# A long convolution beside a gated MLP: the taps' product on GpSimd, and the head, third stage and last stores rearranged

## The chip, the core and the metric

The kernel runs on one core of a Trainium2 chip. The metric is the device time in microseconds of one execution; the median of three runs is compared. Each core has five engines that run their own instruction queues in order and wait for one another by semaphores: TensorE (PE, matmuls from SBUF into PSUM), VectorE (DVE), ScalarE (ACT), GpSimd (POOL) and SyncE (SP, which here only issues DMAs).

## What is computed

```python
def reference(A_q, A_k, A_v, A_shift_k, A_ssm_k, A_ssm_D, B_x, B_w_gate, B_w_up, B_w_down):
    def _A_ref(q, k, v, shift_k, ssm_k, ssm_D):      # S = 2048, D = 640, ks = 4
        k_shift = sum(k_pad[:, t:t + S, :] * shift_k[:, ks - 1 - t] for t in range(ks))
        kv = k_shift * v
        y = irfft(rfft(kv, 2 * S) * rfft(ssm_k, 2 * S))[:S]      # a causal convolution over the sequence
        y = y + kv * ssm_D
        return q * y
    def _B_ref(x, w_gate, w_up, w_down):              # F = 1728
        return (sigmoid(x @ w_gate) * (x @ w_up)) @ w_down
    x = A_q
    xn = _layernorm(x, axis=-1)
    return x + _A_ref(xn, A_k, A_v, A_shift_k, A_ssm_k, A_ssm_D) + _B_ref(xn, B_w_gate, B_w_up, B_w_down)
```

(shortened: the sum over `t` is a loop, and the transforms are 2-d calls on a unit axis). All inputs are bf16.

## The kernel before

Two parts that share little run interleaved, so that TensorE always has something to do.

**The MLP.** The 2048 rows are 16 row blocks of 128 (`m`), in four groups of four (`tr`). The blocks are loaded into `acc`, which also collects the result. For each block the statistics are taken (`bn_stats` on VectorE, L629, or sums on ScalarE, L636 and L642), the rows are normalised into `xn` (L673, L675), transposed to `xnT` (on TensorE for groups 0 and 1, by DMA for 2 and 3), multiplied with the gate and up weights (`rec_first` at L732 for the first 256 columns of the first group, `rec_fc` at L751 for the rest), passed through sigmoid and product (`rec_evac`) into `hT`, and multiplied with the down weights (`rec_down`, L765). The step `fin` (L771) adds the down product from PSUM to `acc`.

**The convolution.** It is done as a transform in two factors over the sequence, in ten steps (`idx` 0 to 9, 16 channels of each of 4 groups a step). In each step, `rec_kv` makes the taps' sum on VectorE: two tap products of 2048 columns (L485), a sum of 2048 (L490), one of 1024 (L491), and then the product of the taps with `v` (L495, kind `ttkt`), which lands in one of two `kvt` buffers. `rec_st1` transforms `kvt` (and the filter `ht`) on TensorE (L513) and copies the result from PSUM to `T` (kind `ev_T`). `rec_st2` is the second factor (L533, `ev_S` into `S`), `rec_prod` the complex product on VectorE (L556 to L564; in steps 3 to 9 a swap DMA brings the halves together), `rec_st3` the inverse of the second factor (L574, `ev_V` into V, which is in VX). When all ten steps are through, `rec_st4` does the last factor (L604), and `ymul`, `yadd` (L611, L612) multiply with the normalised rows and add to `acc`. At the end `store` (L620) writes `acc` out.

**The order.** The code records some 900 operations with what they read and write. `ORDER` is a list, written out by hand or by a planner, of the numbers of these operations; they are emitted in just this order, each on its own engine, so it sets the order on every engine and on both DMA-issuing queues (SyncE and ScalarE). An operation that can run on two engines runs on the first that is listed unless its number is in `ON_DVE`. Buffers (`SLOTS`) are given out in the order of emission.

**Places that the change touches.** `sraw`, the raw shift taps, is one of the `EARLY` names, which live in the part of the tile VX that V's second half takes over later; it is written on every 32nd partition by `load_shift` (memset at L407, DMA at L408) and read by the matmuls `csh` (L414). The scratch of `bn_stats` (`bss`) and the normalised rows `xns` lie there too. `Ab` holds the constants of the third stage: three variants, of which `rec_st3` uses the third. `ROWS` names the steps in which the product `ttkt` writes rows: it reads with a step of 16 elements and writes contiguously.

Of the kernel before, what the change touches and what calls it, by code (L numbers as in the profile page):

```python
# [13 lines left out]
U16 = mybir.dt.uint16  # L14
I32 = mybir.dt.int32
ACT = mybir.ActivationFunctionType
# [3 lines left out]
DM = 640  # L20
# [22 lines left out]
def _dft_tables():  # L43
# [20 lines left out]
    A = np.zeros((2, K2, 3, N2, 2))  # L64
    A[0, :, 0, :, 0], A[0, :, 0, :, 1] = c, s
    A[1, :, 0, :, 0], A[1, :, 0, :, 1] = -c, -s
    A[:, :, 1, :, 0], A[:, :, 1, :, 1] = -s[None], c[None]
    A[0, :, 2, :, 0], A[0, :, 2, :, 1] = c, s
    A[1, :, 2, :, 0], A[1, :, 2, :, 1] = -s, c
    A = np.concatenate([A.reshape(P, 3 * N2 * 2), F], axis=1)  # L70
# [50 lines left out]
]  # L121
ON_DVE = [
    48, 98, 100, 104, 134, 135, 136, 137, 142, 145, 260, 325, 427, 439, 451, 474, 479, 486, 498, 503, 777, 826, 831,
    864, 867, 870, 873, 874, 875, 877, 878, 879, 880, 883, 886, 887, 888, 889, 890, 891, 892, 893, 894, 895
# [7 lines left out]
class _Plan:  # L132
# [47 lines left out]
    def table(self):  # L180
        other = set(ON_DVE)
        for i in ORDER:
            o = self.ops[i]
            o.on = [e for e in ("PE", "ACT", "DVE", "SP") if e in o.engs][i in other]
        return [self.ops[i] for i in ORDER]
# [45 lines left out]
def kernel(  # L231
# [17 lines left out]
    oq4 = out.flatten_outer_dims().rearrange("(n q m) d -> q n m d", q=4, m=NQ)  # L249
# [22 lines left out]
    At = cst.tile([P, 6 * N2 + 2 * K1], U16, name="At")  # L272
    Mb = Mt.bitcast(F16)
    Atb = At.bitcast(F16)
    Ab = Atb[:, 0:6 * N2].rearrange("p (x n) -> p x n", x=3)
    Fb = Atb[:, 6 * N2:6 * N2 + 2 * K1]
# [36 lines left out]
    EARLY = {"xn0", "xn1", "xn2", "xn3", "sraw", "jk", "ident", "FR", "w0_4", "bs0", "bs1", "bs2", "bs3"}  # L313
# [56 lines left out]
    ROWS = tuple(range(10))  # L370
    TD = 1
    FIN2 = (15,)
# [31 lines left out]
    def load_shift():  # L404
        b, c = "sraw", "csh"
        sr = lambda: tl[b].rearrange("p m d -> p (m d)")
        plan.op("memset_s", {"DVE": lambda: nc.vector.memset(sr()[:, 0:4 * CG], 0.0)}, w=[(b, 0)], alloc=[(b, "xq")])  # L407
# [65 lines left out]
    def rec_kv(idx):  # L473
# [8 lines left out]
        def mul(t, r):  # L482
# [12 lines left out]
        dve("ttkt", 1024, lambda: nc.vector.tensor_tensor(out(), f(tl[a][:, 0]), f(tl[vb][:, :, j0:j0 + 2 * JS]), ALU.mult),  # L495
            r=[(a,)] + vr_, w=[(o,)], alloc=[(o, "kvt")])
# [69 lines left out]
    def rec_st3(idx):  # L566
        half, sub = divmod(idx, NSUB)
        V, Z, S_ = f"V{half}", f"P{idx}", f"S{idx}"
        for b in range(2):
            c = f"c3_{idx}_{b}"  # L570

            def f(b=b, c=c):
                for j in range(JS):
                    nc.tensor.matmul(tl[c][:, j // 4, 128 * (j % 4):128 * (j % 4) + 128], lhsT=tl[S_][:, b, 0, j, :],  # L574
                                     rhs=Ab[:, 2, :], start=True, stop=True)
            z = (sub, b) == (0, 0)
            pe("st3", 8, f, r=[(S_, "z"), (S_, "q"), ("A",)] + ([] if z else [(V, "a")]),
               w=[(c,)] + ([(V, "a")] if z else []), alloc=[(c, "c")] + ([(V, "VA" if half == 0 else "VB")] if z else []))
            co = 2 * sub * JS + b
            ev("ev_V", 1024, lambda co=co: tl[V].rearrange("p n r d -> p (n r) d")[:, :, co:co + 2 * JS - 1:2],  # L580
               lambda c=c: tl[c].rearrange("p a n -> p (a n)").rearrange("p (j n) -> p n j", j=JS),
               r=[(c,)], w=[(V, sub, b)])
# [311 lines left out]
```

## Time and profile before

| what | us |
|---|---|
| median of 3 runs | 242.99 (242.56 to 243.24) |
| the profiled execution | 242.73 |
| its span (first to last instruction) | 240.7 |
| TensorE busy | 230.0 (granted clock 0.997) |
| VectorE busy | 194.3 |
| ScalarE busy | 182.3 |
| GpSimd busy | 0.7 |
| product `ttkt` (L495): 10 instructions on VectorE | 2.16 each |
| eviction `ev_V` (L355 into VX) on ScalarE | 1.30 each |
| `fin` (L771): 640 columns, 320 columns | 0.82, 0.49 |

A line of the profile names line, engine, operation and tiles (output first), then count, busy time, mean duration in ns, and after the last bar the idle time of the engine before these instructions with what ended it. In the chain and in timelines the first two numbers are start and duration in us. The 2.03 us between the span and the time of the execution lie outside of the program's own instructions.

### The profile page before, as it was taken

The page shows a single profiled execution, that of the slowest core. Times are in us where ns is not written, and L with a number is a line of the kernel's source. Part 1 is how long each engine was busy: PE and PEld are TensorE (multiplying, and loading weights), DVE is VectorE, ACT ScalarE, POOL GpSimd, SP SyncE. Part 2 cuts the span into 40 slices and gives each one's busy share as a digit, 9 for nine tenths or more (in the row PEclk, how much of TensorE's full clock was granted, in tenths as well). Part 3 has the DMA queues.
Part 4 walks back from the last instruction along what each step waited for, and adds up shares of the span by engine and source line. Part 5 has one row for each costly group of instructions (what it writes and reads, how often), then busy time and mean ns, then how long its engine had stood idle before and what let it go on. Part 6 is the DMA issues. An engine that isn't in the chain of part 4 may idle for free.

```text
span 240.7 us, 8296 instructions
## 1 busy us (share of the span) xinstructions
PE 230.0 (96%) x3678; PEld 139.5 (58%) x3706; DVE 194.3 (81%) x253; ACT 182.3 (76%) x271; POOL 0.7 (0%) x6
## 2 busy tenths in 40 slices
PE   7699999999999999999999999999999999999992
PEld 2574445775445546768655655567774644556671
DVE  3622584299999999989999999899988884889991
ACT  5756899933999999999898999998658666684110
POOL 1000000000000000000000000000000000000000
PEclk9999999999999999999999999999999999999998
DMA  6899999999996886758888477496065688711446
GB/s 178 277 267 276 247 319 147 147 155 198 186 187 151 246 110 124 124 86 121 149 148 203 147 197 250 131 182 190 3 147 177 151 252 272 221 62 42 107 107 190
DMA packets 89115, 41.37 MB, mean 172 GB/s; under 512 B 66544, under 2 KB 85816, under 8 KB 88888
## 3 DMA queue, kind: packets, MB, share of 16 engines
q1 hardware_dynamic: 88360, 39.41, 75.4%
q10 hardware_dynamic: 720, 1.43, 2.1%
q8 instruction: 29, 0.48, 0.9%
q14 instruction: 6, 0.05, 0.1%
HBM read 30.61 MB, written 5.24 MB: 149 GB/s over the span
## 4 chain that ended last, share of the span: by engine, by line
PE 87%; DMA 4%; DVE 3%; issue 2%; ACT 2%; ACTq 0%; DVEq 0%; SPq 0%
PE psa L751 44%; PE psa L765 25%; PE psa L533 7%; PE psa L574 3%; PE psa L513 3%; PE psa L604 2%; PE psa L732 2%; DMA P<-S 2%; DMA acc<-in_A_q_dram 1%; DMA VX<-in_A_shift_k_dram 1%; PE psa L695 1%; DVE VX L629 1%; DVE S L562 1%; DVE P L556 1%; DVE S L564 1%
## 5 line engine op out<-in xcount | busy, mean ns | idle before, releaser
L751 PE MATMUL psa<-xnT,w 128*128 128x512 bf16 x320 | 78.1, 380 | 1.4 <-issue 0.5
L765 PE MATMUL psa<-wd,hT 128*128 128x320 bf16 x448 | 66.1, 300 | 0.2 <-ACT S L355 0.2
L765 PEld LDWEIGHTS <-hT 128*128 128x128 bf16 x448 | 42.2, 98 | 17.0 <-issue 0.2
L751 PEld LDWEIGHTS <-w 128*128 128x128 bf16 x340 | 31.8, 98 | 34.8 <-issue 0.5
L355 ACT CAST S<-psa 128x1024 bf16<-128x1024 f32 (+1 forms) x41 | 39.6, 1047 | 7.2 <-PE psa L533 4.7
L751 PE MATMUL psa<-xnT,VX 128*128 128x512 bf16 x172 | 41.0, 380 | 0.5 <-issue 0.2
L716 ACT ACTIVATE sig<-psa 128x512 bf16<-128x512 f32 x52 | 31.4, 616 | 11.2 <-PE psa L751 4.9
L751 PEld LDWEIGHTS <-VX 128*128 128x128 bf16 x180 | 16.9, 98 | 19.1
L355 ACT CAST hT<-psa 128x512 bf16<-128x512 f32 x33 | 19.5, 607 | 9.5 <-PE psa L751 9.4
L355 ACT CAST T<-psa 128x1024 bf16<-128x1024 f32 (+1 forms) x21 | 21.0, 1056 | 2.7 <-PE psa L513 2.7
L355 ACT CAST VX<-psa 128x1024 bf16<-128x1024 f32 x17 | 21.6, 1298 | 1.1 <-PE psa L574 0.8
L533 PEld LDWEIGHTS <-Mt 64*128 64x128 f16 x1280 | 19.6, 95 | 4.4 <-issue 4.3
L495 DVE TENSOR_TENSOR kvt<-ta,vt 128x1024 bf16<-128x1024 bf16 x10 | 21.6, 2160 | 0.1
L533 PE MATMUL psa<-T,Mt 64*128 64x64 bf16 x1280 | 21.2, 190 | 0.0
L722 DVE TENSOR_TENSOR hT<-sig,psa 128x512 bf16<-128x512 bf16 x16 | 10.7, 681 | 12.4 <-PE psa L751 8.2
L358 ACT ACTIVATE T<-psa 128x1024 bf16<-128x1024 f32 x20 | 20.1, 1056 | 0.0
L771 DVE TENSOR_TENSOR acc<-psa,acc 128x640 bf16<-128x640 f32 (+1 forms) x17 | 13.1, 780 | 7.3 <-PE psa L765 7.0
L719 DVE TENSOR_TENSOR hT<-sig,hT 128x512 bf16<-128x512 bf16 x36 | 14.9, 420 | 4.0 <-ACT sig L716 3.3
L564 DVE TENSOR_TENSOR S<-P 64x2048 bf16<-64x2048 bf16 x10 | 12.2, 1222 | 0.3
L563 DVE TENSOR_TENSOR S<-S 64x2048 bf16<-64x2048 bf16 x10 | 12.2, 1220 | 0.3
L490 DVE TENSOR_TENSOR ta<-ta,P 128x2048 bf16<-128x2048 bf16 x10 | 12.3, 1233 | 0.1
L485 DVE TENSOR_TENSOR P<-kt,sT 128x2048 bf16<-128x2048 bf16 x10 | 12.2, 1223 | 0.2
(83 smaller groups left out, 211.0 us busy)
## 6 DMA issues: line engine op xcount, KB each, us to landing
w<-in_B_w_up_dram SPq DMA_DIRECT2D x7, 640.0 KB, 6.1
w<-in_B_w_gate_dram SPq DMA_DIRECT2D x6, 640.0 KB, 5.0
P<-S SPq DMA_DIRECT2D x14, 256.0 KB, 3.9
kt<-in_A_k_dram SPq DMA_DIRECT2D x8, 320.0 KB, 6.5
vt<-in_A_v_dram SPq DMA_DIRECT2D x8, 320.0 KB, 7.3
xnd<-VX SPq DMA_DIRECT2D x4, 640.0 KB, 6.4
acc<-in_A_q_dram SPq DMA_DIRECT2D x12, 160.0 KB, 7.7
ht<-in_A_ssm_k_dram SPq DMA_DIRECT2D x8, 192.0 KB, 6.1
```

What stands on the lines that cost most here:

```text
L355: fa = lambda: nc.scalar.copy(out=out_fn(), in_=in_fn())
L358: fa = lambda: nc.scalar.activation(out_fn(), in_fn(), ACT.Copy, scale=scale)
L485: dve("tap", 2048, lambda: nc.vector.tensor_tensor(tl[t][:], bass.AP(k().tensor, k().offset, [k().ap[0], [HALF, 2], [HALF, N2], [1, 2 * JS]]),
L490: dve("tap", 2048, lambda: nc.vector.tensor_tensor(tl[a][:], tl[a][:], tl[b][:], ALU.add), r=[(b,)], w=[(a,)])
L495: dve("ttkt", 1024, lambda: nc.vector.tensor_tensor(out(), f(tl[a][:, 0]), f(tl[vb][:, :, j0:j0 + 2 * JS]), ALU.mult), r=[(a,)] + vr_, w=[ ...
L533: nc.tensor.matmul(tl[c][:, b, 64 * kk:64 * kk + 64], lhsT=Mb[rows, k, 64 - 64 * r:192 - 64 * r], rhs=tl[T][rows, 2 * k + r].rearrange("p ...
L564: dve("pr", 2048, lambda: tt(X()[64:P], Q()[0:64], Q()[64:P], ALU.add), r=[(S_, "z"), (Z, 0), (Z, 1)], w=[(S_, "q")])
L716: act("sig", 512, lambda: nc.scalar.activation(tl[sg][:], pv(0), ACT.Sigmoid), r=[pk(0)], w=[(sg,)], alloc=[(sg, "sig")])
L719: dve("gmul2", 512, lambda: nc.vector.tensor_tensor(hT[:, fc, :], tl[sg][:], hT[:, fc, :], ALU.mult), r=[(sg,), (hk, fc, 0)], w=[(hk, fc)])
L751: nc.tensor.matmul(tl[c][:], lhsT=w()[:, k, o:o + P], rhs=tl[X][:, k, :], start=(k == 0), stop=(k == NC - 1))
L765: nc.tensor.matmul(tl[p_][:, i, 0:320], lhsT=hT[:, fc, t4 * P:(t4 + 1) * P], rhs=wd[:, fc, 320 * i:320 * i + 320], start=(fc == 0), stop=( ...
L771: dve("fin", 320 * (i1 - i0), lambda i0=i0, i1=i1, m=m, p_=p_: nc.vector.tensor_tensor(acc[:, m, 320 * i0:320 * i1].rearrange("p (a d) -> ...
```

## The change

1. **Product on GpSimd.** `ROWS` becomes empty and `ttkt` is recorded for GpSimd (`nc.gpsimd.tensor_tensor`). Both inputs are now read contiguously, and the output is written with a step of 64 elements. 
2. **Head.** `sraw` no longer lies in VX: it takes a `kvt` buffer. It is no `EARLY` name any more.
3. **Third stage.** `rec_st3` takes four column groups of both halves in each of its two parts, instead of eight of one half, so that `ev_V` writes runs of eight neighbouring elements instead of every second one. The unused variants of `Ab` go, and the table's DMA shrinks from 896 to 384 bytes a partition.
4. **Last stores.** `CUT` splits the down product of block 13 into 480 and 160 columns, and that of block 15, as before, into 320 and 320. The stores are cut to match: block 12; block 13 from column 160 with block 14; block 15; and the first 160 columns of block 13 by themselves.
5. **New order.** `ORDER` and `ON_DVE` are new lists.

```diff
 ORDER = [
-    8, 5, 7, 0, 6, 45, 4, 15, 1, 13, 73, 66, 17, 14, 16, 72, 11, 74, 25, 46, 77, 78, 75, 76, 92, 97, 9, 79, 18, 19,
+    8, 5, 7, 0, 6, 45, 4, 15, 1, 16, 72, 14, 11, 13, 17, 9, 77, 46, 73, 74, 25, 78, 75, 76, 79, 80, 92, 83, 82, 97,
...
 ON_DVE = [
-    48, 98, 100, 104, 134, 135, 136, 137, 142, 145, 260, 325, 427, 439, 451, 474, 479, 486, 498, 503, 777, 826, 831,
-    864, 867, 870, 873, 874, 875, 877, 878, 879, 880, 883, 886, 887, 888, 889, 890, 891, 892, 893, 894, 895
+    37, 48, 98, 100, 102, 135, 136, 137, 139, 140, 141, 142, 144, 145, 147, 195, 271, 288, 333, 337, 369, 371, 441,
+    451, 455, 459, 469, 479, 498, 504, 555, 557, 559, 724, 772, 794, 804, 821, 865, 867, 868, 870, 871, 873, 874,
+    875, 876, 880, 881, 882, 883, 884, 886, 887, 888, 889, 892, 893, 894
 ]
...
-            o.on = [e for e in ("PE", "ACT", "DVE", "SP") if e in o.engs][i in other]
+            o.on = [e for e in ("PE", "ACT", "DVE", "POOL", "SP") if e in o.engs][i in other]
...
-    EARLY = {"xn0", "xn1", "xn2", "xn3", "sraw", "jk", "ident", "FR", "w0_4", "bs0", "bs1", "bs2", "bs3"}
+    EARLY = {"xn0", "xn1", "xn2", "xn3", "jk", "ident", "FR", "w0_4", "bs0", "bs1", "bs2", "bs3"}
...
-    ROWS = tuple(range(10))
+    ROWS = ()
     TD = 1
-    FIN2 = (15,)
+    CUT = {13: ((160, DM), (0, 160)), 15: ((0, 320), (320, DM))}
...
-        sr = lambda: tl[b].rearrange("p m d -> p (m d)")
-        plan.op("memset_s", {"DVE": lambda: nc.vector.memset(sr()[:, 0:4 * CG], 0.0)}, w=[(b, 0)], alloc=[(b, "xq")])
+        sr = lambda: tl[b].rearrange("p j b n -> p (j b n)")
+        plan.op("memset_s", {"DVE": lambda: nc.vector.memset(sr()[:, 0:4 * CG], 0.0)}, w=[(b, 0)], alloc=[(b, "kvt")])
...
         f = (lambda t: t.rearrange("p n (j b) -> p j b n", b=2)) if rows else (lambda t: t.rearrange("p n (j b) -> p n j b", b=2))
         out = lambda: tl[o][:] if rows else tl[o].rearrange("p j b n -> p n j b")
-        dve("ttkt", 1024, lambda: nc.vector.tensor_tensor(out(), f(tl[a][:, 0]), f(tl[vb][:, :, j0:j0 + 2 * JS]), ALU.mult),
-            r=[(a,)] + vr_, w=[(o,)], alloc=[(o, "kvt")])
+        eng, tt = ("DVE", nc.vector.tensor_tensor) if rows else ("POOL", nc.gpsimd.tensor_tensor)
+        plan.op("ttkt", {eng: lambda: tt(out(), f(tl[a][:, 0]), f(tl[vb][:, :, j0:j0 + 2 * JS]), ALU.mult)}, info=(1024,),
+                r=[(a,)] + vr_, w=[(o,)], alloc=[(o, "kvt")])
...
-                for j in range(JS):
-                    nc.tensor.matmul(tl[c][:, j // 4, 128 * (j % 4):128 * (j % 4) + 128], lhsT=tl[S_][:, b, 0, j, :],
-                                     rhs=Ab[:, 2, :], start=True, stop=True)
+                for x in range(2):
+                    for j in range(4):
+                        nc.tensor.matmul(tl[c][:, x, 128 * j:128 * j + 128], lhsT=tl[S_][:, x, 0, 4 * b + j, :],
+                                         rhs=Ab, start=True, stop=True)
...
-            co = 2 * sub * JS + b
-            ev("ev_V", 1024, lambda co=co: tl[V].rearrange("p n r d -> p (n r) d")[:, :, co:co + 2 * JS - 1:2],
-               lambda c=c: tl[c].rearrange("p a n -> p (a n)").rearrange("p (j n) -> p n j", j=JS),
+            co = 2 * sub * JS + JS * b
+            ev("ev_V", 1024, lambda co=co: tl[V].rearrange("p n r d -> p (n r) d")[:, :, co:co + JS].rearrange("p n (j x) -> p n j x", x=2),
+               lambda c=c: tl[c].rearrange("p x (j n) -> p n j x", j=4),
...
-            for i in range(2):
+            for i, (d0, d1) in enumerate(CUT.get(m, ((0, 320), (320, DM)))):
...
-                            nc.tensor.matmul(tl[p_][:, i, 0:320], lhsT=hT[:, fc, t4 * P:(t4 + 1) * P],
-                                             rhs=wd[:, fc, 320 * i:320 * i + 320],
+                            nc.tensor.matmul(tl[p_][:, i, 0:d1 - d0], lhsT=hT[:, fc, t4 * P:(t4 + 1) * P],
+                                             rhs=wd[:, fc, d0:d1],
...
-    dma(lambda e: e.dma_start(At[:], Adram.ap()), 128, 896, w=[("A",)])
+    dma(lambda e: e.dma_start(At[:], Adram.ap()), 128, 384, w=[("A",)])
...
-    store(12, 14)
-    store(14, 15)
-    store(15, 16, 0, 320)
-    store(15, 16, 320, 640)
+    store(12 * DM, 13 * DM)
+    store(13 * DM + 160, 15 * DM)
+    store(15 * DM, 16 * DM)
+    store(13 * DM, 13 * DM + 160)
```

In the order, operations 9 to 12 are the loads of the first gate and up weights, 13 to 16 those of row blocks 2 and 3, 17 a first use of ScalarE's square root with its table load, 46 the DMA of the shift taps, 72 and 73 the statistics of block 0, and 82 and 83 those of block 2. The numbers of the four-way stores and of the last additions shift by one, since block 13 now has two of these. On VectorE the new lists put 234 operations instead of 228, on ScalarE 241 instead of 256, on GpSimd 10.

More of the change, by code (lines that the diff above doesn't have):

```diff
@@ L63, in _dft_tables @@
     c, s = np.cos(ph), np.sin(ph)
[L64 to L70, printed above, removed]
+    A = np.zeros((2, K2, N2, 2))
+    A[0, :, :, 0], A[0, :, :, 1] = c, s
+    A[1, :, :, 0], A[1, :, :, 1] = -s, c
+    A = np.concatenate([A.reshape(P, N2 * 2), F], axis=1)
     t = 64.0 * n1[None, :] + n2[:, None]
@@ L248 @@
     xq4 = A_q.flatten_outer_dims().rearrange("(n q m) d -> q n m d", q=4, m=NQ)
-    oq4 = out.flatten_outer_dims().rearrange("(n q m) d -> q n m d", q=4, m=NQ)
+    oq4 = out.flatten_outer_dims().rearrange("(n q m) d -> q n (m d)", q=4, m=NQ)
     k3 = A_k.flatten_outer_dims().rearrange("(a b) d -> a b d", b=N2)
@@ L271 @@
     Mt = cst.tile([P, K1, 3 * K2], U16, name="Mt")
-    At = cst.tile([P, 6 * N2 + 2 * K1], U16, name="At")
+    At = cst.tile([P, 2 * N2 + 2 * K1], U16, name="At")
     Mb = Mt.bitcast(F16)
     Atb = At.bitcast(F16)
-    Ab = Atb[:, 0:6 * N2].rearrange("p (x n) -> p x n", x=3)
-    Fb = Atb[:, 6 * N2:6 * N2 + 2 * K1]
+    Ab = Atb[:, 0:2 * N2]
+    Fb = Atb[:, 2 * N2:2 * N2 + 2 * K1]
     sT = cst.tile([P, 4, CG], BF16, name="sT")
@@ L614, in rec_st4, with store @@
             r=[(xb, "x")], w=[("cv", u)], c=[("acc", m, q) for m in range(m0, m1) for q in range(4)])
-    def store(m0, m1, d0=0, d1=DM):
-        key = [("fin", m, x) for m in range(m0, m1) for x in range(2) if d0 <= 320 * x < d1] + [
-            ("cv", u) for u in sorted({min(m // 3, 5) for m in range(m0, m1)})]
+    def store(a, b):
+        ms = range(a // DM, -(-b // DM))
+        key = [("fin", m, x) for m in ms for x, (d0, d1) in enumerate(CUT.get(m, ((0, 320), (320, DM))))
+               if DM * m + d0 < b and a < DM * m + d1] + [("cv", u) for u in sorted({min(m // 3, 5) for m in ms})]
         for q in range(4):
-            dma(lambda e, q=q: e.dma_start(oq4[q][:, m0:m1, d0:d1], acc[32 * q:32 * q + 32, m0:m1, d0:d1]), 32,
-                2 * (d1 - d0) * (m1 - m0), True, kind="store", r=key, w=[("out", m0, d0, q)])
+            dma(lambda e, q=q: e.dma_start(oq4[q][:, a:b], acc.rearrange("p m d -> p (m d)")[32 * q:32 * q + 32, a:b]), 32,
+                2 * (b - a), True, kind="store", r=key, w=[("out", a, q)])
     MEAN, VAR, RST, TMP, EPS = range(5)
@@ L760, in rec_down, with f @@
             p_ = f"pd{m}"
-            for i in range(2):
+            for i, (d0, d1) in enumerate(CUT.get(m, ((0, 320), (320, DM)))):
                 for c0, c1 in ((0, 7), (7, 14)):
-                    def f(c0=c0, c1=c1, t4=t4, p_=p_, i=i):
+                    def f(c0=c0, c1=c1, t4=t4, p_=p_, i=i, d0=d0, d1=d1):
                         for fc in range(c0, c1):
-                            nc.tensor.matmul(tl[p_][:, i, 0:320], lhsT=hT[:, fc, t4 * P:(t4 + 1) * P],
-                                             rhs=wd[:, fc, 320 * i:320 * i + 320],
+                            nc.tensor.matmul(tl[p_][:, i, 0:d1 - d0], lhsT=hT[:, fc, t4 * P:(t4 + 1) * P],
+                                             rhs=wd[:, fc, d0:d1],
                                              start=(fc == 0), stop=(fc == NFC - 1))
-                    pe("down", c1 - c0, f, r=[("hT", fc) for fc in range(c0, c1)] + [("wd", fc) for fc in range(c0, c1)] +
+                    pe("down" if d1 - d0 == 320 else f"down{d1 - d0}", c1 - c0, f, r=[("hT", fc) for fc in range(c0, c1)] + [("wd", fc) for fc in range(c0, c1)] +
                        ([("z",)] if c1 == 14 else []), w=[(p_, i)], alloc=[(p_, "c")] if c0 == i == 0 else ())
-            for i0, i1 in (((0, 1), (1, 2)) if m in FIN2 else ((0, 2),)):
-                dve("fin", 320 * (i1 - i0), lambda i0=i0, i1=i1, m=m, p_=p_: nc.vector.tensor_tensor(
-                    acc[:, m, 320 * i0:320 * i1].rearrange("p (a d) -> p a d", d=320), tl[p_][:, i0:i1, 0:320],
-                    acc[:, m, 320 * i0:320 * i1].rearrange("p (a d) -> p a d", d=320), ALU.add),
+            for i0, i1, d0, d1 in ([(i, i + 1, *CUT[m][i]) for i in range(2)] if m in CUT else [(0, 2, 0, DM)]):
+                dve("fin", d1 - d0, lambda i0=i0, i1=i1, d0=d0, d1=d1, m=m, p_=p_: nc.vector.tensor_tensor(
+                    acc[:, m, d0:d1].rearrange("p (a d) -> p a d", a=i1 - i0), tl[p_][:, i0:i1, 0:(d1 - d0) // (i1 - i0)],
+                    acc[:, m, d0:d1].rearrange("p (a d) -> p a d", a=i1 - i0), ALU.add),
                     r=[(p_, i) for i in range(i0, i1)], w=[("fin", m, i) for i in range(i0, i1)], c=[("acc", m, q) for q in range(4)])
@@ L856 @@
         rec_down(tr)
-    for m0, m1 in ((0, 3), (3, 6), (6, 9), (9, 12)):
-        store(m0, m1)
-    store(12, 14)
-    store(14, 15)
-    store(15, 16, 0, 320)
-    store(15, 16, 320, 640)
+    for a in (0, 3, 6, 9):
+        store(DM * a, DM * a + 3 * DM)
+    store(12 * DM, 13 * DM)
+    store(13 * DM + 160, 15 * DM)
+    store(15 * DM, 16 * DM)
+    store(13 * DM, 13 * DM + 160)
     plan.emit(plan.table(), make)
```

78 rows, old and new, of the table ORDER are left out of this document.

## The prediction

> **What bounds the kernel now.** The first look is at the page's busy shares and the chain that ended last.
>
> ```profile
> span 240.7 us, 8296 instructions
> PE 230.0 (96%) x3678; PEld 139.5 (58%) x3706; DVE 194.3 (81%) x253; ACT 182.3 (76%) x271; POOL 0.7 (0%) x6
> PE 87%; DMA 4%; DVE 3%; issue 2%; ACT 2%; ACTq 0%; DVEq 0%; SPq 0%
> ```
>
> TensorE is the bound and GpSimd is empty. The table by stages (5 us each) says where TensorE is not full: the first 9 us and the last 5 us. Between 10 and 235 us no stage has it below 4.76 of 5.00, and the granted clock is 1.00. Does "busy" hide waits? The chain in order of time gives best rates: 0.216 us for a gate or up matmul (31 in 6.69), 0.136 for a down one (7 in 0.95), 0.0154 and 0.0107 in stages two and one, 0.056 in stage three, 0.010 in stage four. Times their counts (492, 448, 1280, 640, 160, 512), with 7.5 us for transposes, first tile and small ones, that is 215 us. The work runs from 8.98 (the first tile's first matmul) to 236.06, 227.1 us. The other 12 us lie at some 140 changes from one kind of matmul to another, about 0.09 us each; only a few tenths are waits with a named releaser. So an edit gains by letting TensorE start earlier or by shortening what follows its end; in the middle it can only lose.
>
> The chain's start shows who holds TensorE back:
>
> ```profile
> 4.16 0.90 DVE VX L629 x2
> 5.08 0.22 DVE st L631
> 5.32 2.20 DMA VX<-in_A_shift_k_dram
> 7.59 0.89 DVE VX L629 x2
> 8.48 0.06 DVE st L649
> 8.54 0.40 DVE xnT L356
> 8.98 0.72 PE psa L732 x10
> ```
>
> VectorE's statistics of row block 2 (L629, from 7.59) wait for the DMA of the shift taps, whose numbers they don't use. That DMA goes to `sraw`, a view of VX on every 32nd partition, and the statistics' scratch lies in VX too; it starts as the statistics of block 0 end (L631). Behind the waiting statistics is queued the copy of the first transposed block (L356), which the first weight matmuls (L732) need. The transposes were done at 6.80, the normalisation at 6.30.
>
> The end, in the timeline:
>
> ```profile
> 228.23 9.81 SPq L620 DMA_DIRECT2D out_dram<-acc  x16
> 230.18 5.88 PE L765 MATMUL psa<-wd,hT 128*128 128x320 bf16 x42
> 231.34 6.92 ACTq L620 DMA_DIRECT2D out_dram<-acc  x8
> 236.10 0.82 DVE L771 TENSOR_TENSOR acc<-psa,acc 128x640 bf16<-128x640 f32 x1 [1.52 <-PE psa L765]
> ```
>
> After TensorE's last matmul: 0.86 us to the end of a 640-column addition, 1.1 to the end of the last store issue (238.04), 2.7 until the data are out.
>
> The shapes apart, for prices:
>
> ```profile
> L495 DVE TENSOR_TENSOR kvt<-ta,vt 128x1024 bf16<-128x1024 bf16 x10 | 21.6, 2160 | 0.1
> L355 ACT CAST VX<-psa 128x1024 bf16<-128x1024 f32 x17 | 21.6, 1298 | 1.1 <-PE psa L574 0.8
> L771 DVE TENSOR_TENSOR acc<-psa,acc 128x640 bf16<-128x640 f32 x15 | 12.1, 819 | 7.0 <-PE psa L765 6.6
> L771 DVE TENSOR_TENSOR acc<-psa,acc 128x320 bf16<-128x320 f32 x2 | 1.0, 486 | 0.3 <-PE psa L765 0.3
> masks.py:199 POOL TENSOR_SCALAR_AFFINE_SELECT VX<-VX 128x128 bf16<-128x128 bf16 x1 | 0.3, 292 | 0.1
> ```
>
> **Head: -1.1 us.** `sraw` moves to a `kvt` buffer, so the wait on the shift DMA goes. What is late next? The loads of blocks 2 and 3. In the new order ScalarE issues its two before its table load (the second went out at 3.44 in the trace); of SyncE's two, one now goes behind a weight load. Issued by 3.4 at the latest and 3.2 us to landing (the median of SyncE's 80 KB issues here), it is there by 6.6. VectorE is free at 6.30; statistics 0.89 and copy 0.47 end at 7.9. The first matmul now takes gate weights, a load that SyncE moves ahead of shift and table; issued by 4.3 and 3.4 us to landing (the 320 KB row), it is there by 7.7. Start about 7.9 against 8.98. Bounds: 0.3 if the weights, in one queue behind more bytes, land near 8.7; 1.7 if all loads beat VectorE.
>
> **Tail: -0.6 us.** Block 13 is done last and cut into 480 and 160 columns. The last addition shrinks from 0.82 to about 0.32 (0.333 us per 320 columns by the two L771 rows): -0.5. The other additions, of block 15 too, run beside the 14 matmuls of 160 columns. The last four stores carry 40 KB together, not 320, still two a queue: I take 0.1, between nothing and 0.5. TensorE does the same columns, so nothing there; a loss would need block 15's stores to be still in issue (0.37 to 0.42 us each) when the last sum is ready, at most 0.4.
>
> **Changes of kind: +0.2 us.** The list of TensorE's operations in the new order has 145 changes against 143.
>
> **The product on GpSimd: 0 taken.** Off VectorE: 10 x 2.16 = 21.6 us. By the new engine list VectorE takes over 4 normalisations (0.42), 3 copies of transposes (0.49), 2 up copies (0.68), 2+1+3 stage evictions (1.23 to 1.26), 2 small copies, and gives back 2 of 1.15: +10.5, so 194.3 becomes 183.2. ScalarE loses these, and the third stage's evictions now write runs of 8 elements like ev_S (1054 ns against 1298): 182 becomes about 166. Neither sets the end; TensorE's saturation hides both, and without that cover VectorE's 11 us would be the gain.
>
> The new wait: stage one of each step, and the next step's first tap product, which reuses `ta`, wait for GpSimd. No row shows its two-input product. Lower bound, from the select (292 ns for 128 columns against 102 for one): 1.5 ns an element, 1.6 us; upper, two inputs read in turn: 3.2. I take 2.2, nearest the same product on VectorE. The page of the Trainium skill "GPSIMD Engine Reference", section "Performance versus the Vector engine", gives 2.6 cycles an element for two inputs, at 1.2 GHz an estimate of 2.2 us; no run here shows it yet. Behind the product nothing is queued on GpSimd. Between its end and stage one, the trace has 7 to 14 us in steps 0 to 3 (ends at 59.9 and 66.5, stage one at 70.1 and 73.8) and 0.9 to 3.3 in the later ones (129.2 to 130.1; 181.3 to 184.5). So a product of 2.2 fits; 1 us more does not in the later steps.
>
> At table, renamed store slices, the new third-stage operand order: same counts, cost nothing; DMAs off the path hide them.
>
> **Sum.** 242.73 (the profiled execution) - 1.1 - 0.6 + 0.2 = 241.2. It lies 0.26 under the median of the runs, so 241.5 on their scale.
>
> **Rivals.** (1) GpSimd and VectorE exclude each other, slower. From 50 to 195 us VectorE is busy 137.35 of 145. Less 21.6, plus the 10.7 that fall there, it is 126.4, which leaves 18.6. If each product holds up VectorE for its whole 2.2 us, that is 22.0: 3.4 over, and TensorE, which runs in order, waits them out: 244.9. At 3.2 us each it is 13.4 over, of which some 6 operations of 1.2 us that read PSUM (put beside the product in the new order) may take back 7: 247.9. It decides from 1.86 us held per product. The Trainium skill, "SBUF — State Buffer", section "Who interferes with whom", says just this: a VectorE instruction with two SBUF inputs and a GpSimd one that reads SBUF lock each other out whole. The trace can't show it, GpSimd being empty. For: 120 us of VectorE's work are such products and sums. Against: VectorE's order gives up time elsewhere, and the lock costs only where an operand pair is next in line.
> (2) The head's gain is lost: the first weights land near 8.7 and later loads set the pace, and the last stores queue as before. Then 242.73 - 0.3 - 0.2 + 0.2 = 242.4, 242.7 on the runs' scale: no change.
> (3) The wait at 7.59 was not for the shift DMA but for the row loads; the loads' new places then give about half, 242.1. It counts with the forecast.
>
> **Numbers.** Forecast with (3): 0.58. Rival (1): 0.30. Rival (2): 0.12. A run of this kernel can tell about 0.3%, 0.7 us, from no change: faster is under 242.3, slower over 243.7. The predicted time is 241.5. The lower end takes the head at 1.7, the tail at 1.0 and no extra changes: 240.3, and 0.5 less for fewer pauses at changes: 239.8. The upper end takes in (1) at 2.2 us with a further 1 us of waits at the later steps' stage one: 246.0.
>
> **What would show it.** Right: first L732 matmul near 7.9; last addition 160 columns, 0.3 us; no stage between 10 and 230 us with TensorE under 4.7; GpSimd products near 2.2 us. Wrong: VectorE's tap sums or products stretched beyond 1.23 us beside a GpSimd product, waits of stage one or of VectorE's `ta` on GpSimd, TensorE gaps from 100 to 200 us; or a start still at 8.5 with a DMA of weights as releaser.

## The result and the profile after

The changed kernel takes **273.22 us** (median of four runs, 271.62 to 276.00) beside 242.92 for the kernel before: ratio 1.1217, interval 1.1169 to 1.1266. The forecast was 241.5, its upper end 246.0. One of its four runs (276.00), and one of e2's below (289.38), counts as slow; the ratios and the sums below go by the others, whose medians are 272.04 and 284.61.

The page of the changed kernel, the lines that answer to the first three of before (span, busy time of each engine, the chain that ended last by engine):

```profile
span 272.6 us, 8349 instructions
PE 239.3 (88%) x3706; PEld 142.3 (52%) x3706; DVE 215.7 (79%) x259; ACT 170.7 (63%) x256; POOL 50.4 (19%) x16
PE 47%; DVE 32%; DMA 9%; issue 4%; SPq 2%; POOL 2%; ACT 2%; ACTq 0%; DVEq 0%; POOLq 0%
```

VectorE lost ten products of 2.16 us and yet is busier than before (215.7 against 194.3). In the chain it went from 3% to 32%. GpSimd has only 2% of the chain, and TensorE's own waits for its product, in the view of waits (engine and line, what it waited for: us in total, times, longest), are far from the 29 us that were lost:

```profile
PE psa L512 <- POOL kvt L494: 6.4, 3, 3.5
```

The groups with the shapes apart (count, busy us, mean ns, idle before) show both sides; first two of before, then those of the changed kernel:

```profile
L719 DVE TENSOR_TENSOR hT<-sig,hT 128x512 bf16<-128x512 bf16 x36 | 14.9, 420 | 4.0 <-ACT sig L716 3.3
L485 DVE TENSOR_TENSOR P<-kt,sT 128x2048 bf16<-128x2048 bf16 x10 | 12.2, 1223 | 0.2
```

```profile
L494 POOL TENSOR_TENSOR kvt<-ta,vt 128x1024 bf16<-128x1024 bf16 x10 | 49.7, 4973 | 159.0 <-DVE ta L489 96.2
...
L721 DVE TENSOR_TENSOR hT<-sig,hT 128x512 bf16<-128x512 bf16 x36 | 25.5, 725 | 5.1 <-ACT sig L718 4.0 <-ACT hT L353 0.2
L483 DVE TENSOR_TENSOR P<-kt,sT 128x2048 bf16<-128x2048 bf16 x10 | 16.3, 1625 | 0.1
...
L353 ACT CAST VX<-psa 128x1024 bf16<-128x1024 f32 x16 | 16.2, 1017 | 9.6 <-PE psa L574 9.6
L675 DVE TENSOR_SCALAR VX<-acc,st 128x640 bf16<-128x640 bf16 x14 | 13.9, 990 | 0.2
...
L661 DVE TENSOR_SCALAR st<-st 128x8 int32<-128x8 int32 x1 | 4.8, 4766 | 0.0
```

A product on GpSimd takes 4.97 us, not 2.2. On VectorE the means of unchanged instructions rose (1625 ns for a tap product, before 1223; 725 ns for the product L721, before 420 as L719), and one instruction on 8 columns, whose twin for 4 columns takes 170 ns, took 4766. The timeline from 58 us shows why (start, duration; only some of the lines):

```profile
58.84 4.80 POOL L494 TENSOR_TENSOR kvt<-ta,vt 128x1024 bf16<-128x1024 bf16 x1 [57.53 <-DMA vt<-in_A_v_dram]
58.90 4.77 DVE L661 TENSOR_SCALAR st<-st 128x8 int32<-128x8 int32 x1
...
68.14 0.61 PE L512 MATMUL psa<-At,ht 32*128 32x64 f16 x32 [3.09 <-DVE ht L468]
...
69.89 0.69 DVE L715 TENSOR_TENSOR hT<-sig,psa 64x512 bf16<-64x512 bf16 x1
70.00 4.80 POOL L494 TENSOR_TENSOR kvt<-ta,vt 128x1024 bf16<-128x1024 bf16 x1 [6.36 <-DVE ta L489]
70.61 4.37 DVE L675 TENSOR_SCALAR VX<-acc,st 128x640 bf16<-128x640 bf16 x1
```

Twice VectorE's instruction begins while the product runs and ends 0.03 or 0.18 us after it (58.84 + 4.80 = 63.64; 58.90 + 4.77 = 63.67). The product L715, one of whose inputs lies in PSUM, ran its usual 0.69 us across a GpSimd product's start. Behind the held instruction VectorE's queue stands, and TensorE, which needs something further down in it (`ht` of L468), waits 3.09 us. Then a second loss: the table by windows of 2 us (window, TensorE busy, weight loads, VectorE, ScalarE, GpSimd, granted clock, DMA share, GB/s).

```profile
66.00:68.00 2.00, 0.00 (x0) 0.00 (x0) 2.00 (x4) 1.66 (x3) 0.00 (x0) 0.88 1.09 125
68.00:70.00 2.00, 1.86 (x36) 0.95 (x37) 1.94 (x4) 1.22 (x2) 0.00 (x1) 0.50 1.61 143
70.00:72.00 2.00, 2.00 (x8) 0.68 (x6) 1.97 (x2) 1.31 (x2) 2.00 (x1) 0.77 0.52 45
```

After TensorE's idle time its granted clock is 0.50 in the next window; it is back at 1.00 from 72 us until the next long wait (3.33 us, to 88.19), behind which it is 0.50 again. The mean over the span is 0.974.

Head and tail, which the prediction counted as gains, in the timeline after:

```profile
7.07 0.89 DVE L631 BATCH_NORM_STATS2 VX<-acc 128x6 f32<-128x320 bf16 x2 [0.76 <-DMA acc<-in_A_q_dram]
...
7.88 0.47 DVE L354 COPY xnT<-psa 128x640 bf16<-128x640 bf16 x1
...
8.40 0.72 PE L734 MATMUL psa<-xnT,VX 128*128 128x128 bf16 x10 [0.92 <-DVE xnT L354]
...
269.01 0.33 DVE L773 TENSOR_TENSOR acc<-psa,acc 128x160 bf16<-128x160 f32 x1 [0.48 <-PE psa L767]
```

The wait for the shift taps is gone; the statistics now wait for the row loads themselves and the first weight matmul starts at 8.40 instead of 8.98. (In the nine traces with this head it starts at 8.40 to 8.68, in the six with the head of before at 8.85 to 9.10: some 0.4 us earlier.) From TensorE's end (268.98) to the span's end it is 3.6 us, before 4.6.

### The profile page after: what moved, and what is told of

Read it like the earlier page. It is cut to its first block, busy times and chain, and to the rows that moved or that the text cites. A ratio compares the mean times of both kernels' runs of the same rounds, so it can differ in the third digit from the quotient of the medians.

```text
span 272.6 us, 8349 instructions
## 1 busy us (share of the span) xinstructions
PE 239.3 (88%) x3706; PEld 142.3 (52%) x3706; DVE 215.7 (79%) x259; ACT 170.7 (63%) x256; POOL 50.4 (19%) x16
## 4 chain that ended last, share of the span: by engine, by line
PE 47%; DVE 32%; DMA 9%; issue 4%; SPq 2%; POOL 2%; ACT 2%; ACTq 0%; DVEq 0%; POOLq 0%
PE psa L753 25%; PE psa L767 14%; DVE P L483 4%; DVE hT L721 4%; DMA VX<-in_B_w_up_dram 3%; DVE S L562 3%; DVE ta L488 3%; DVE ta L483 3%; PE psa L532 3%; DMA xnd<-VX 2%; DMA P<-S 2%; DVE S L561 2%; POOL kvt L494 2%; DVE VX L675 2%; PE psa L604 2%
## 5 line engine op out<-in xcount | busy, mean ns | idle before, releaser
L494 POOL TENSOR_TENSOR kvt<-ta,vt 128x1024 bf16<-128x1024 bf16 x10 | 49.7, 4973 | 159.0 <-DVE ta L489 96.2
L767 PE MATMUL psa<-wd,hT 128*128 128x320 bf16 (+2 forms) x448 | 65.7, 299 | 0.0
L753 PE MATMUL psa<-xnT,VX 128*128 128x512 bf16 x180 | 44.5, 398 | 1.6 <-ACT sig L718 1.2
L721 DVE TENSOR_TENSOR hT<-sig,hT 128x512 bf16<-128x512 bf16 x36 | 25.5, 725 | 5.1 <-ACT sig L718 4.0
L353 ACT CAST VX<-psa 128x1024 bf16<-128x1024 f32 x16 | 16.2, 1017 | 9.6 <-PE psa L574 9.6
L356 ACT ACTIVATE T<-psa 128x1024 bf16<-128x1024 f32 x18 | 17.8, 1024 | 2.9 <-PE psa L512 2.9
L773 DVE TENSOR_TENSOR acc<-psa,acc 128x640 bf16<-128x640 f32 (+3 forms) x18 | 13.4, 747 | 7.8 <-PE psa L767 7.6
L562 DVE TENSOR_TENSOR S<-S 64x2048 bf16<-64x2048 bf16 x10 | 16.2, 1617 | 0.3
L574 PE MATMUL psa<-At,S 128*128 128x128 f16 x160 | 11.9, 219 | 5.1 <-DVE S L563 2.6
L483 DVE TENSOR_TENSOR P<-kt,sT 128x2048 bf16<-128x2048 bf16 x10 | 16.3, 1625 | 0.1
L574 PEld LDWEIGHTS <-S 128*128 128x128 bf16 x160 | 10.0, 98 | 8.6 <-DVE S L563 5.5
```

Source lines behind the costliest of these rows:

```text
L353: fa = lambda: nc.scalar.copy(out=out_fn(), in_=in_fn())
L356: fa = lambda: nc.scalar.activation(out_fn(), in_fn(), ACT.Copy, scale=scale)
L483: dve("tap", 2048, lambda: nc.vector.tensor_tensor(tl[t][:], bass.AP(k().tensor, k().offset, [k().ap[0], [HALF, 2], [HALF, N2], [1, 2 * JS]]),
L494: plan.op("ttkt", {eng: lambda: tt(out(), f(tl[a][:, 0]), f(tl[vb][:, :, j0:j0 + 2 * JS]), ALU.mult)}, info=(1024,), r=[(a,)] + vr_, w=[(o ...
L562: dve("pr", 2048, lambda: tt(X()[0:64], X()[0:64], X()[64:P], ALU.subtract), r=[(S_, "p")], w=[(S_, "z")])
L574: nc.tensor.matmul(tl[c][:, x, 128 * j:128 * j + 128], lhsT=tl[S_][:, x, 0, 4 * b + j, :], rhs=Ab, start=True, stop=True)
```

## The experiments

Three theories at the outset, by the letters of the expectations: **L**, the long product holds VectorE, whole, whenever its next instruction is of the kind that is held; **W**, only the waits of stage one and of the tap products for a product of 4.8 us; **O**, the new order and the evictions that moved to VectorE are slow in themselves. "Step" below is the distance between neighbouring elements of an operand; "no steps" still reads `v` in runs of 16 neighbours.

| run | base | product | us | ratio to before, interval |
|---|---|---|---|---|
| e1_dve_rows | after | VectorE, reads with steps of 16 elements (sum of the taps) and 80 (`v`), 2.16 us | 257.32 | 1.0626 [1.0593, 1.0658] |
| e2_dve_step | after | VectorE, writes with a step of 64 elements, 4.75 us | 285.22 | 1.1737 [1.1680, 1.1794] |
| e3_pool_alone | before | GpSimd as in after, 5.12 us | 261.92 | 1.0805 [1.0773, 1.0836] |
| e4_lock_only | before | VectorE as before, and one on GpSimd for nobody, 5.09 us | 279.90 | 1.1547 [1.1507, 1.1586] |
| e5_wait_only | after | none; GpSimd fills memory for 5 us | 246.97 | 1.0204 [1.0064, 1.0344] |
| e6_pool_contig | after | GpSimd, no steps, 2.39 us | 249.69 | 1.0317 [1.0242, 1.0391] |
| e7_pool_rows | after | GpSimd, reads with steps as in e1, 4.71 us | 274.09 | 1.1325 [1.1254, 1.1395] |
| e8_no_product | after | none; GpSimd fills memory for 1 us | 240.77 | 0.9938 [0.9901, 0.9975] |
| e13_wait_short | after | none; GpSimd fills memory for 2 us | 240.08 | 0.9880 [0.9841, 0.9919] |
| e11_dve_contig | after | VectorE, no steps, 0.69 us | 241.81 | 0.9957 [0.9927, 0.9986] |
| e9_head | before | as before; new place of `sraw`, with a load order of its own | 242.09 | 0.9967 [0.9935, 0.9999] |
| e14_tail3 | before | as before; tail of the change | 241.43 | 0.9950 [0.9924, 0.9977] |
| b4_old_order | after | VectorE as before; head of e9, old order in the middle, tail of the change | **240.31** | 0.9898 [0.9866, 0.9931] |

Where a row says "none", or names a product without the step that its place in the transform asks for, the kernel leaves out or alters that part of the computation.

**Is it the engine, the step or the order?** e1: `ROWS = tuple(range(10))` and the product on VectorE. e2: the product as in after, on VectorE.

> The changed kernel with only the product put back on VectorE in its old row form (ROWS of all ten steps); head, third stage, last stores, engine list and new order stay. Theory L (the product takes 4.8 us on GpSimd and holds up VectorE's own operand pairs for that long): with GpSimd empty the time falls to 241.2, between 240 and 243, the first weight matmul stays near 8.0 us and the last addition at 0.33 us. Theory W (only the wait for the 4.8 us product counts, VectorE's holding is incidental): the same, 240 to 243. Theory O (the new order and the moved evictions are themselves slow): over 262.

> The changed kernel with the product on VectorE in the new form: contiguous reads, writes with a step of 64 elements. L and W: 239.5 to 243, with the product between 1.2 us (one element a cycle as the evictions show) and 2.2 us (as the row form); if the step of the write is what makes GpSimd slow, a stretched product here too would hint at it. O: over 262.

Group lines of the product, e2 and then e7 (the row form on GpSimd) and e6 (no steps):

```profile
L494 DVE TENSOR_TENSOR kvt<-ta,vt 128x1024 bf16<-128x1024 bf16 x10 | 47.5, 4746 | 0.2
```

```profile
L496 POOL TENSOR_TENSOR kvt<-ta,vt 128x1024 bf16<-128x1024 bf16 x10 | 47.1, 4714 | 162.0 <-DVE ta L489 130.3 <-DMA vt<-in_A_v_dram 25.9 <-PE psa L755 5.8
```

```profile
L494 POOL TENSOR_TENSOR kvt<-ta,vt 128x1024 bf16<-128x1024 bf16 x10 | 23.9, 2388 | 159.4 <-DVE ta L489 149.1 <-PE psa L753 10.4
```

The write with a step of 128 bytes makes the product 4.75 us on VectorE too; reading with steps of 32 and 160 bytes leaves it at 2.16 there and costs 4.71 on GpSimd; without steps GpSimd takes 2.39 in the mean. So GpSimd's price of the prediction was that of another form. And e1 and e2 missed: L and W had expected about the time of before for both. The new order has put more evictions and normalisations onto VectorE (205.3 us busy in e1 against 194.3 before), and with the product back on it there is no room. The table by windows of e1:

```profile
60.00:100.00 40.00, 33.68 (x601) 17.39 (x600) 39.09 (x47) 30.76 (x44) 0.00 (x0) 1.00 0.80 145
```

TensorE 33.7 of 40 beside a VectorE at 39.1, nothing held. To see whether it goes with the length, e11 has the product on VectorE without steps.

> The changed kernel with its new order, the product on VectorE reading and writing all its columns one after the other (its columns then lie in another order, so the output is another one). Nothing is held and VectorE carries one short instruction for it, 0.6 to 1.2 us. Same order with the product at 2.16 us on VectorE took 257.3, with it left out 240.8. If VectorE's load in this order is what cost e1 its 16 us, and goes with the product's length: 243 to 248. If the order has room for about a microsecond for each product: 240.8 to 242. If the order itself were the cause, whatever the length: over 250.

241.81. So the new order is not slow by itself: it carries 0.69 us a product, and the next 1.47 us of each (14.7 in ten) cost 15.5 us of time. O holds only where VectorE carries more than in e11, and in the change it does so only by being held.

**Waiting or holding?** e3 is the kernel before with only the product moved, in the old order. e4 keeps before's product and adds to each a GpSimd product (`kvt` squared, written with a step of 80 elements over columns of `v` that are no longer needed), for which no engine that computes waits (one load of `v` waits 8.0 us for it; TensorE waits 0.4 us for such a load).

```diff
+            nc.gpsimd.tensor_tensor(tl[vb][:, :, j0:j0 + 2 * JS].rearrange("p n c -> p c n"), k, k, ALU.mult)
```

> The kernel before with one part of the change alone: the product on GpSimd, written with the step; order, head, third stage and stores as before. L: VectorE's instruction behind each product start is held some 3 to 4 us, ten times, against 21.6 us of relief, and nothing in this order stands ready beside it: 262 to 280. W: the product ends 2.6 us later than on VectorE, and the last six steps have 0.9 to 3.3 us to spare: 245 to 253. O: 241 to 245.

> The kernel before with the product on VectorE as before, and behind each one an extra GpSimd product of the same size and step (the finished product squared, written over columns of v that nobody reads any more), for which no instruction of the chain waits. L: holding alone, without relief and without a wait: 10 holds of 3 to 4.8 us on an engine that had 7.6 us to spare between 50 and 195 us, so 262 to 290. W: 242 to 244, since nothing waits for it. O: 242 to 244.

e4's timeline, then its groups:

```profile
60.98 4.56 POOL L498 TENSOR_TENSOR vt<-kvt 128x1024 bf16<-128x1024 bf16 x1 [59.67 <-DVE kvt L496]
61.65 4.49 DVE L485 TENSOR_TENSOR ta<-kt,sT 128x2048 bf16<-128x2048 bf16 x1
```

```profile
L498 POOL TENSOR_TENSOR vt<-kvt 128x1024 bf16<-128x1024 bf16 x10 | 50.9, 5087 | 165.6 <-DVE kvt L496 165.6
L485 DVE TENSOR_TENSOR ta<-kt,sT 128x2048 bf16<-128x2048 bf16 x10 | 28.7, 2866 | 0.1
```

A GpSimd product that nobody needs costs 37 us. VectorE's busy time rises by 34.0 (194.3 to 228.3). That is holding, with before's order and code for the rest, and without the wait for the product. In e3 VectorE also waits 20.1 us itself for GpSimd (the next tap product reuses `ta`), and the time comes to 261.9, at the lower end that L had given: moving the product alone already loses 19.5 us.

e5, e13 and e8 are the other half: stage one waits for GpSimd, but GpSimd reads nothing from SBUF. The product is replaced by a copy of 64 columns on VectorE and 5, 2 or 1 memsets of 0.96 to 0.98 us on GpSimd.

```diff
+            nc.vector.tensor_copy(k[:, 0:64], tl[a].rearrange("p x n d -> p (x n d)")[:, 0:64])
+            for _ in range(5):
+                nc.gpsimd.memset(k, 0.0)
```

> The changed kernel with the product left out: a VectorE copy of 64 columns, then five GpSimd memsets of the kvt buffer, for which stage one waits as it waited for the product (the taps' product with v is not computed). GpSimd is busy about 4.6 us a step but reads nothing. W (the wait counts): stage one still waits some 4.6 us after the taps' sum, so 262 to 273. L (the holding of VectorE counts): VectorE is never held, so 240 to 250, unless a VectorE tensor_scalar between SBUF buffers is held by a write too. O (the order itself): over 255 as with the product back on VectorE (257.3).

> The changed kernel with the product left out but for a 64-column VectorE copy and one GpSimd memset of the kvt buffer, 0.9 us (the taps' product with v is not computed). What the new order gives if the product is nearly free on both engines: L: 239 to 243, the head and tail gains of the prediction with nothing held. O: the order and its moved evictions cost by themselves, over 250.

> The changed kernel with the product left out; in its place a copy of 64 columns on VectorE and two GpSimd memsets of the product's buffer, about 2.15 us in all, for which stage one waits; GpSimd reads nothing from SBUF. The prediction took such a wait at nothing: 240.5 to 241.3, as with the product left out (240.8). The product on GpSimd that reads and writes in order (2.1 to 2.4 us) took 249.7: if waiting made half of its loss or more, this takes over 244.

The waits in e5 (engine and line, what it waited for: us in total, times, longest), and one of its groups:

```profile
PEld L517 <- POOL kvt L498: 8.0, 6, 3.0
PE psa L517 <- POOL kvt L498: 5.7, 5, 2.8
```

```profile
L726 DVE TENSOR_TENSOR hT<-sig,hT 128x512 bf16<-128x512 bf16 x36 | 14.5, 421 | 6.5 <-ACT sig L723 5.3 <-ACT hT L353 0.2
```

Memsets hold none of the products (421 ns, as without them); the one row they stretch is a copy of 3072 columns (L425), 1.67 us beside a memset and 0.95 in e8. Waiting 2.1 us costs nothing (240.08 beside 240.77), waiting 5.1 us costs 6.9 (246.97, from two runs, 245.68 and 248.26). So W is about a fifth of the loss, and the 6.4 us of TensorE's waits in the changed kernel agree.

**Holding at the forecast price.** e6 and e7, both in the new order.

> The changed kernel with the GpSimd product written contiguously instead of with the step (the columns of kvt then stand in another order than stage one takes them for, the rest is the same work). If the step sets the length, as the 4.75 us on VectorE in the last comparison suggests, the product falls from 4.8 to between 1.6 and 3.2 us, and with L the time to 245 to 262; if it is GpSimd's own rate for two inputs, the product stays at 4.5 to 4.8 us and the time at 270 to 275. W: 250 to 262 in the first case.

> The changed kernel with the GpSimd product in the old row form: reads with a step of 16 elements, contiguous writes. If only writing with a step is slow, the product takes 1.6 to 3.2 us and the time is as with contiguous writes; if GpSimd reads with a step as slowly, it stays at 4 us or more and the time at 265 to 280.

e7 is about as slow as the changed kernel; its product is nearly as long. e6 differs from e13 by holding only: both have their product or its stand-in done after some 2 us, and in e6's trace no engine waits for the product. The tables by windows of e13 and of e6:

```profile
60.00:100.00 40.00, 39.47 (x799) 22.55 (x804) 38.28 (x56) 37.63 (x52) 7.61 (x8) 1.00 0.89 160
...
180.00:220.00 40.00, 39.58 (x644) 22.14 (x634) 31.66 (x39) 24.54 (x35) 0.00 (x0) 1.00 0.59 179
```

```profile
60.00:100.00 40.00, 34.79 (x625) 18.36 (x633) 38.80 (x54) 32.16 (x45) 6.65 (x4) 1.00 0.75 138
...
180.00:220.00 40.00, 39.58 (x625) 23.27 (x629) 30.99 (x35) 24.94 (x34) 2.12 (x1) 1.00 0.63 186
```

From 60 to 100 us, where VectorE is at 38.3 of 40 without any product, holding takes 4.7 us from TensorE: three of VectorE's stretches there are held some 5.1 us together (L675 at 67.60, L721 at 75.50, L483 at 83.80). From 180 to 220, where VectorE has 8 us free, the one product that falls there takes nothing. Over the span VectorE is held 13.5 us (197.6 in e6, less the 184.1 that e13 has without its 1.8 of stand-in copies) and the time rises by 9.6.

**Head and tail by themselves.** e9 has before's order with the change's place for `sraw` and a sequence of the first 21 operations that is neither before's nor the change's: ScalarE issues its two late row loads ahead of its table load, as in the change, but SyncE's two both go ahead of the first weights (the change puts one behind them), and the first gate weights stay behind the table and the shift taps. Three runs were meant for the tail: e10_tail (the cut blocks), e12_tail2 (the change's own sequence of additions and stores, on the old positions) and e14_tail3 (the last 90 operations of the change's order, behind before's). b1_old_order, b3_old_order, b4_old_order and b5_old_order are the changed code with the product on VectorE in row form, the head of e9, before's order in the middle and those tails (the last with 130 operations). So where the expectations speak of the change's head, it is e9's that was run; the change's own was not run by itself.

> The kernel before with the change's head alone (the state of the first stage lies in a product buffer, so that w_up's first tile takes the earlier place among the loads); the product stays on VectorE in row form, the order elsewhere as before. The step of the prediction's head: the first weight matmul (line 734 or its counterpart) starts 1.0 to 1.3 us earlier than in the kernel before, and the time falls by 0.8 to 1.3 us, to about 241.3 beside 242.4. The theory that the gain is lost again further on (rival 2): the matmul starts as much earlier and the time stays within 0.3 of 242.4. Since leaving the product out gave 240.8 with head and tail together, a fall of less than 0.5 here would put that gain down to the tail or to the lighter VectorE.

> The kernel before with the change's tail alone (last two blocks cut unevenly, last addition of 160 columns, the stores that go with it); head, product and middle as before. The step of the prediction's tail: last addition 0.32 instead of 0.82 us, time from TensorE's end to the span's end 0.5 to 0.6 shorter, and the time falls by 0.3 to 0.8, to about 241.8. The rival: the stores, one more on the queue, end as late as before, and the time stays within 0.2 of 242.4.

> The kernel before with the change's tail alone, now with its own sequence of the last additions and stores and its split over the two queues. The step of the prediction's tail: the span ends 3.2 to 3.4 us after the last addition, and the time falls by 0.3 to 1.0, to about 242.0 beside 242.6. The rival, that the stores end as late as before: within 0.3 of the kernel before.

> The kernel before, with the last 90 operations of the order (the last units of the fourth stage, the additions, the stores) taken from the change. The step of the prediction's tail: the last addition is one of 160 columns, the span ends 3.2 to 3.4 us after it, and the time falls by 0.3 to 1.0 beside 242.7. If the tail is worth nothing by itself and the run with the product left out won its 1.7 elsewhere: within 0.3 of the kernel before.

e9: the first weight matmul starts at 8.19 and the time falls by 0.7; the interval, 0.9935 to 0.9999, only just leaves out no change. In the four b runs, with the same head, the start is at 7.59 to 8.37. e10 gained nothing (243.29, ratio 1.0022 [0.9993, 1.0052]): its last stores were split otherwise over the two queues and ended 5.2 us after the last addition. e12 lost (246.18, 1.0145 [1.0099, 1.0190]): there the last unit of the fourth stage is added only 0.3 us before TensorE's end (at 235.16 of 235.49), and behind it nine stores of ScalarE's queue begin, which are issued until 241.5. With the whole end of the change's order (e14) the time falls by 1.2; in the profiled execution, the longest of its twelve (243.38), the last addition ends at 238.26 of 241.5. So the cut alone gains nothing; the gain comes with the whole end of the order, by these traces through its queues and the earlier last unit.

> The changed kernel's code with the product on VectorE in row form (2.16 us) and with the order of the kernel before in the middle; its head, its tail and its table for the third stage stay. If holding and the product's place cost all of what the change lost, and head and tail are gains of 1.1 and 0.6: about 240.7, between 240.2 and 241.5, which beats both kernels. If the head's gain is lost further on: 241.8 to 242.4. If the new order were better than the old one apart from the product, this would be no faster than 240.8, the run with the product left out.

> The run b1_old_order (head, tail, third stage of the change, product on VectorE in row form, the middle in the order of the kernel before), with the tail mended in the same way. b1_old_order took 241.8 with its span ending 5.2 us after the last addition. If the tail's store queues were the loss: 0.8 to 2.0 less than b1_old_order, 239.8 to 241.0. If the time is set by the stores' bytes: as b1_old_order, 241.5 to 242.

> The changed kernel's head, third stage and last 90 operations, its product on VectorE in row form, and the order of the kernel before between. b1_old_order took 241.8 with stores that ended 5.2 us after the last addition. With head and tail both worth what the prediction says: 240.2 to 241.3, faster than both kernels. If only one of them is: 241.3 to 242.2.

> As b4_old_order with the last 130 operations from the change. The same forecast, 240.2 to 241.3; a difference of more than 0.7 between the two would say that it matters where the two orders are joined, and not only what the last stores do.

b1 took 241.79 (0.9958 [0.9933, 0.9983]) and b3 244.65 (1.0076 [1.0042, 1.0111]), with the tails of e10 and e12; b5 241.21 (0.9950 [0.9925, 0.9974]). b4 is the fastest that does the whole computation: 240.31, 2.3 under the kernel before and some 32 under the changed one. The end of its timeline:

```profile
234.80 0.32 DVE L765 TENSOR_TENSOR acc<-psa,acc 128x160 bf16<-128x160 f32 x1 [0.47 <-PE psa L759]
```

Its span ends at 238.4, 3.3 after that. Why b5 is 0.9 slower than b4 was not followed up.

## Why the prediction was wrong

**The step that failed is "The product on GpSimd: 0 taken".** It held two statements, and both fell.

*The price.* 2.2 us, between 1.6 and 3.2, was worked out from a GpSimd row that writes contiguously. The change says "written with a step", and the step was given no price. Measured: 2.39 without steps (e6), so the middle was near for that form, and 4.97 with it, beyond the upper end by 1.8. The rows that would have warned were of another engine and other operands, but in the trace before: VectorE's product, 2.16 with read steps, and its sum of 1024 columns without one (L491), 0.69; e11 has the product itself at 0.69. The estimate of 2.2 us from the Trainium skill, "GPSIMD Engine Reference", "Performance versus the Vector engine", agrees with e6 and doesn't speak of a written step.

*The holding.* Rival (1), given 0.30, is the mechanism. The Trainium skill's page "SBUF — State Buffer", section "Who interferes with whom", has it: a VectorE instruction with two SBUF inputs contends with a GpSimd instruction that reads SBUF and not with one that only writes, and a copy or `tensor_scalar` in a two-port mode contends with GpSimd as well. The traces agree: beside a product, L675 ran until 0.18 us behind the product's end and L483 until 0.57 (5.29 us from 91.65, the product 4.83 from 91.54); beside the memsets of e5 the two-input products were not held (L721's counterpart 421 ns), and a copy was. But the rival's price was too small as well, and the range left out even its own 247.9 at 3.2 us. At 2.2 us it gave 244.9, and e6 at 2.39 took 249.7. Its 18.6 us of room were a mean over 145 us, while from 60 to 100 us there was 1.7 us of room in e13, and e6 lost there almost all that it was held. "It decides from 1.86 us held per product" is refuted: e6 held 1.35 per product and lost 9.6 in all.

*The sum as measured*, all in the new order: 240.1 with a wait of 2.1 us and nothing held; 6.9 for waiting 5.1 us instead (e5); another 25 for holding at 4.97 us (272.0 less 247.0), with VectorE held 31.6 us (215.7 less 184.1). The latter two were one term of 0; they are split by difference, so what each would cost without the other is not told by this sum. Against e13, TensorE idles 25 us more (33.3 against 8.2), and its busy time is 9.8 higher, where the dips of the granted clock come in.

**The other terms.**
- Head: -1.1 forecast with a start at 7.9. Measured: 8.40 in the changed kernel, and over the traces with its head some 0.4 us gained at the start, less than half of the term. What was late next was named (the row loads), but the statistics behind them start at 7.07, not 6.6. e9's 8.19 and -0.7 us belong to its own load order.
- Tail: -0.6 forecast (bounds 0.1 to 1.0). The last addition is 0.33 as forecast; e14 has -1.2, of which the traces show 1.0 after TensorE's end (4.6 to 3.6 us); the other 0.2 is within the noise.
- Waits at 2.2 us "fit": right (e13).
- VectorE's other work: 183.2 forecast, 185.9 in e13 with 1.8 of stand-in copies. ScalarE: 166 forecast, 170.7 measured. `ev_V`: 1054 ns forecast, 1017 measured.
- Changes of kind: +0.2 can't be told apart; e13, everything but the product, is at 0.988 of before, 2.7 us under it where the prediction's sum had 1.5.

## What to carry to other kernels

An instruction that goes to another engine takes its access pattern with it: price the pattern first, from a row that has the same step on the same operand, and where no row has it, leave the upper end open. Ask what the new engine shares with those already at work; time in which a queue is held can be paid almost whole wherever that queue is full and feeds the bound engine (here some 5.1 us held, 4.7 lost), so compare it with the room in each stretch, not with the mean over the kernel. And the parts that gain are worth cutting out of a change that loses (b4, with e9's head and the change's third stage and tail: 2.3 us).

## What the runs showed of the hardware that was not expected

- Steps cost differently by engine and by side: 1024 bf16 products, with a written step of 128 bytes, take 4.75 us on VectorE and 4.97 on GpSimd; with read steps of 32 and 160 bytes 2.16 on VectorE and 4.71 on GpSimd; without steps 0.69 and 2.39.
- A `tensor_scalar` on 8 columns of 32-bit numbers is held as long as one on 640 (4.77 us and 4.37).
- TensorE's granted clock fell to 0.50 after some 3 us without a matmul. The Trainium skill, "TensorE: Matmul & The Clock Gate", section "HAM oscillation — how this bites in real kernels", warns of gaps above about 3.4 us; the trace agrees in kind, but at a shorter gap, 3.09 us between the matmuls at 65.0 and 68.1. A gap of 2.66 us in e6 (before 88.02) left the clock at 1.00.
- The same order takes 241.8, 257.3 or 284.6 us as VectorE's product takes 0.69, 2.16 or 4.75: 10.6 and 10.5 us for each us of a product that occurs ten times. Above 0.69 us all of it is paid.
